# First two tiles' output projection inside the attention's last steps, in the banks of the maxima; the last head group's copies by whole bank

## The chip, the cores and the metric

The kernel runs on one core of a Trainium2 chip. The metric is the device time of one execution in microseconds (us); a figure for the kernel is the median of several executions. Five engines work in parallel: TensorE (PE, with PEld for its weight loads), VectorE (DVE), ScalarE (ACT), GpSimd (POOL) and SyncE (SP), which here issues all DMAs of the stretch that matters. Each engine takes its instructions in the order in which they are written for it.

## The reference

The reference is a transformer block on 2048 tokens with 640 features: sliding window attention with 32 heads of 20 features and a window of 256, then a gated MLP whose gate mixes tokens.

```python
qkv = (layernorm(x) @ wqkv)                      # 32 heads of 20
scores = einsum("bhqd,bhkd->bhqk", q, k) * 20 ** -0.5
p = softmax(where(0 <= i - j < 256, scores, -1e9))
h = x + einsum("bhqk,bhkd->bhqd", p, v) @ wo
z = gelu(layernorm(h) @ w_in); z1, z2 = halves(z)
g = w_sp @ layernorm(z2) + b_sp                  # over tokens
out = h + (z1 * g) @ w_out
```

## The kernel before

The work is fp32 in quality: operands are split into a high and a low part (hi, lo), and each product takes three matmuls (hi·hi, hi·lo, lo·hi). Tokens lie in 16 tiles of 128. The order of the instructions on PE, DVE, ACT and SP is that of the code; only POOL is scheduled by the framework.

The attention runs as 128 steps `u`: eight groups `g` of four heads, and in a group 16 blocks of 128 keys. Step `s` of the loop holds, four times (`hh`, one for each head of the group):

- `max_item` for step `s + 16` (scores for the row maxima; PE fills a bank, DVE reduces it into `junk`), as long as there are steps left, so it is missing in the last 16;
- `score_item` for step `s`: PE fills a bank with scores, ACT takes the exponential into `pt` (line 392), and after the fourth head POOL masks `pt` (lines 394 and 397);
- at `hh` 1 and 3 `pv_item` for step `s - 2`: PE multiplies `pt` with V into a PSUM tile `pv` (line 415), one tile for each 512 tokens of a group, two buffers. After every second key block one half (256 tokens) of a `pv` tile is final; it is copied to `ot` by ACT (line 427) or DVE (line 429) and stored to `o_d` in HBM (line 430). Row 20 of each head holds the softmax sums.

PSUM has eight banks: two for `pv`, six as `bank0` to `bank5` in two rings. Ring 1 (three banks) is that of the maxima; when these end, one of its banks goes to ring 2, the scores'. The other two stand idle from then on.

In the last steps a generator `proj_early`, advanced once a step, prepares the output projection: `load_o(j)` loads tiles 2j and 2j+1 of the attention's result from `o_d` into `m1` (line 157, four DMAs) and the sums into `rs` (line 152); `inv` takes the reciprocals (line 192), `norm_o` multiplies (line 162), `split_o` makes hi (a cast, line 168) and lo (a subtraction, line 171), and `load_x2` loads the residual rows `xh` (line 141). For tokens from 512 on the sums are inverted once for all by `inverse_sums`, one generator for each 512 tokens: it loads the sums into `inv` (line 367), takes the reciprocals (line 371) and stores them to `r_d` (line 372), from which `rs` is loaded later.

The projection of a tile (`proj_o`, line 100) is 30 matmuls. For tiles 0 and 1 it is issued in the two steps after the last score, in new PSUM tiles `wo_ps`, opened when the six banks are closed. After the loop, step `i` of the next stage projects tile `i` on PE, then transposes the normalised rows of tile `i - 2` (`turn_h`, `ht_ps`, line 825); DVE adds the residual (`add_h`, line 1198) and takes the statistics (line 1204), POOL three small operations (lines 85 to 87), and ACT writes the normalised rows `hn` (line 91).

Much later, `second_gate(p)` (p from 0 to 7) runs the second half of the token mixing: PE products `g` (line 1036), to which DVE adds what `first_gate` had left in `g_d`. The load of `g_d[p]` into the row `gi` is issued with the pair's first product.

Of the kernel before, what the change touches and what calls it, by code (L numbers as in the profile page):

```python
# [7 lines left out]
F32 = mybir.dt.float32  # L8
# [3 lines left out]
OP = mybir.AluOpType  # L12
# [3 lines left out]
P = 128  # L16
# [18 lines left out]
def block_kernel(ctx, tc, x, wqk, wv, wo, w_in, wsp, bsp, w_out, out):  # L35
# [5 lines left out]
    def pool(stack, name, **kw):  # L41
        return stack.enter_context(tc.tile_pool(name=name, bufs=1, reuse_waits="tile", **kw))
# [96 lines left out]
    def load_x2(i):  # L139
        hs[i] = mem["xh"][i % 5]  # L140
        nc.sync.dma_start(hs[i], x[i * P:(i + 1) * P, :])

    def load_o(j, sums=False):

        t = slice(2 * j * P, (2 * j + 2) * P)
        ot, rs = m1(j % 2 * 2 * D, KD, 2 * P), mem["rs"][j % 2]
        for i in range(2):
            ots[2 * j + i] = (ot[:, :, i * P:(i + 1) * P], rs[:, i * P:(i + 1) * P])

        def load_rs(sums=False):  # L150
            base, step = (o_d[:, DH, t], 32 * S) if sums else (r_d[:, t], S)
            nc.sync.dma_start(rs, bass.AP(tensor=base.tensor, offset=base.offset, ap=[[0, 4], [step, H], [1, 2 * P]]))

        if sums:
            load_rs(True)
        for d in range(4):
            nc.sync.dma_start(ot[32 * d:32 * d + 32], o_d[:, d:4 * KD:4, t])
        return load_rs

    def norm_o(i):  # L160
        ot, rs = ots[i]
        nc.vector.tensor_tensor(out=ot, in0=ot, in1=rs[:, None, :].to_broadcast([P, KD, P]), op=OP.mult)

    def split_o(i, on_dve=False):
        ot, _ = ots[i]
        hi, lo = ots[i] = mem["osp"][i % 3]
        if on_dve:
            nc.vector.tensor_copy(out=hi, in_=ot)
        else:
            nc.scalar.activation(hi, ot, AF.Copy)  # L170
        return lambda: nc.vector.tensor_tensor(out=lo, in0=ot, in1=hi.bitcast(F32), op=OP.subtract)

    def proj_o(i, ps):
        osp = ots.pop(i)
        wo_s = mem["wo"]
        gemm(ps, HD, [lambda k, p=p: osp[p][:, k, :] for p in range(2)],
             [lambda k, j, p=p: wo_s[p][:, k, j * HD:(j + 1) * HD] for p in range(2)], KD)
        return ps

    def proj_early():  # L180
# [22 lines left out]
        lo = split_o(0, True)  # L203
        load_x2(1)
        yield
        lo()
        norm_o(1)
        load_x2(2)
        yield
        split_o(1, True)()  # L210
        rs = load_o(2)
        yield
        inv(1)
        load_x2(3)
        yield
        load_x2(4)
        norm_o(2)
        lo = split_o(2, True)
        yield
        lo()  # L220
        norm_o(3)
        yield
        yield
        rs()


    with ExitStack() as ab:
# [50 lines left out]
        def s2_tile():  # L278
            return s_tile(2)
# [80 lines left out]
        def inverse_sums(t0, n):  # L360
            t = mem["inv"][len(inverse) % 2][:, :n // 4]

            def rows(d, step):
                return bass.AP(tensor=d.tensor, offset=d.offset, ap=[[step, H], [n // 4, 4], [1, n // 4]])

            yield
            nc.sync.dma_start(t, rows(o_d[:, DH, t0:t0 + n], 32 * S))
            yield
            yield
            yield  # L370
            nc.vector.reciprocal(out=t, in_=t)
            nc.sync.dma_start(rows(r_d[:, t0:t0 + n], S), t)
            yield
# [26 lines left out]
        def pv_item(u):  # L400
            g, kb = divmod(u, NT)
            pt = p_tiles.pop(u)
            a, e = kb * P, min(S, kb * P + 384)
            mid = (a // 512 + 1) * 512 if a // 512 < (e - 1) // 512 else a + 192
            for a, b in ((a, min(mid, e)), (mid, e)):
                if a >= b:
                    continue
                c = a // 512
                first = (g, c) not in pv_tiles
                if first:  # L410
                    pv_tiles[g, c] = pv_tile(f"pv{g}_{c}")
                ps = pv_tiles[g, c]
                for hh in range(4):
                    v0 = 21 * (4 * g + hh)
                    nc.tensor.matmul(ps[32 * hh:32 * hh + 32, a - 512 * c:b - 512 * c],  # L415
                                     v_sb[:, kb, v0:v0 + 32], pt[:, hh, a - kb * P:b - kb * P],
                                     start=first, stop=(kb == 4 * c + 3), skip_group_check=True,
                                     tile_position=(0, 32 * hh))
                if b < e:
                    yield  # L420
            c = kb // 4
            for j in (kb // 2 % 2,) if kb % 2 else ():
                ps = pv_tiles.pop((g, c)) if j else pv_tiles[g, c]
                ot = tmp3.tile([P, 256], F32, tag="ot", bufs=6, name=f"ot{g}_{c}_{j}")
                src, e = ps[:, 256 * j:256 * j + 256], c * 512 + 256 * j
                if u >= NU - 2 or j == 0 and u < NU - LEAD:
                    nc.scalar.activation(ot, src, AF.Copy)
                else:
                    nc.vector.tensor_copy(out=ot, in_=src)  # L429
                nc.sync.dma_start(o_d[4 * g:4 * g + 4, :, e:e + 256].rearrange("h d t -> (h d) t"), ot)  # L430
            if g == 7 and kb % 4 == 3 and c:
                inverse.append(inverse_sums(c * 512, 512))
# [200 lines left out]
        b1.close()  # L633
        tmp3 = pool(x01, "tmp3", side="right")
        early, pre_ps = None, []
        for s in range(NU + 2):
            if s % NT == 0 and s < 6 * NT:
                ld = load_stack(s // NT + 2)
            for _ in range(1 + s % 2):
                next(ld, None)  # L640
            u1 = s + LEAD
            for hh in range(4):
                if u1 < NU:
                    max_item(u1 // NT, u1 % NT, hh)
                if s < NU:
                    score_item(s, hh)
                if hh == 1 and u1 % 8 == 0 and s <= NU - LEAD:
                    rows = max_rows((u1 - 8) // NT, (u1 - 8) % NT // 8)
# [24 lines left out]
            for f in inverse:  # L673
                next(f, None)
        for _ in early:
            pass


    psK = ctx.enter_context(ExitStack())
# [152 lines left out]
    def at(n, f):  # L832
        later.setdefault(n, []).append(f)
# [289 lines left out]
    def second_gate(p):  # L1123
# [71 lines left out]

    def add_h(i):
        h3 = hs[i].rearrange("p (a b) -> p a b", a=2)
        nc.vector.tensor_tensor(out=h3, in0=pre_ps.pop(0)[:, :, :HD], in1=h3, op=OP.add)
        nc.sync.dma_start(h_d[i], hs[i])

    def bn_h(i):
# [94 lines left out]
```

## Time and profile before

| | us |
|---|---|
| three runs | 1128.23, 1132.79, 1138.03 |
| median | 1132.79 |
| profiled execution | 1131.8 |
| its span, first to last instruction | 1130.1 |

The profile gives PE 1095.6 us busy (97% of the span), DVE 725.6, ACT 567.3 and POOL 313.0, with 28703 instructions. It comes as a page and as answers to questions on the trace. A row of the timeline has the start in us from the span's start, the time busy, the engine, the line, the operation, the tiles (out<-in), and in brackets the idle time before it with what ended it. SPq rows are DMA issues. A row of the windows has, for each engine, busy us and instructions, then the granted TensorE clock as a share of full speed, the busy share of the DMA engines and GB/s. A row of the chain of waits has a start, a length and what the end hung on there.

### The profile page before, as it was taken

Reading aid. Unit: us, or ns where it says so; the run is one execution under the profiler, and the core shown is the slowest. Engines: PE = TensorE matmul, PEld = TensorE weight load, DVE = VectorE, ACT = ScalarE, POOL = GpSimd, SP = SyncE. Lnnn points to the kernel's source line nnn. Section 1 sums busy time; section 2 is a strip of 40 time slices with the busy share of each in tenths; the row PEclk is TensorE's granted clock in tenths of the full one; section 3 lists DMA queues with packets and bytes.
Section 4 is the critical chain, followed back from the end, with each engine's and each line's share of the span. In section 5 each row is a group of like instructions: output and inputs, shape, how many; then the busy total and the mean of one; then the engine's idle time right before and its main releaser. Section 6 shows DMA issues by size and latency. Waiting matters only on the chain.

```text
span 1130.1 us, 28703 instructions
## 1 busy us (share of the span) xinstructions
PE 1095.6 (97%) x11180; PEld 988.7 (87%) x11180; DVE 725.6 (64%) x2013; ACT 567.3 (50%) x1198; POOL 313.0 (28%) x477
## 2 busy tenths in 40 slices
PE   8999999999999999699999999999999999999998
PEld 7998887667778877499999999999999899999998
DVE  5541213788989998568777678556358974566542
ACT  4433443248989999635566567333247521222210
POOL 4424444446667667623300012000002100000000
PEclk9999999999999999999999999999999999999999
DMA  6622446555555555679754522233251564444322
GB/s 198 211 70 72 143 136 243 170 179 167 180 181 178 183 177 160 169 214 304 262 177 168 178 90 75 85 122 96 97 170 52 169 187 145 135 136 147 98 76 78
DMA packets 82168, 171.78 MB, mean 152 GB/s; under 512 B 10816, under 2 KB 43072, under 8 KB 78144
## 3 DMA queue, kind: packets, MB, share of 16 engines
q1 hardware_dynamic: 82032, 169.95, 47.0%
q8 instruction: 88, 1.44, 0.6%
q14 instruction: 48, 0.39, 0.1%
HBM read 112.04 MB, written 57.87 MB: 150 GB/s over the span
## 4 chain that ended last, share of the span: by engine, by line
PE 51%; ACT 3%; DVE 2%; DMA 2%; issue 1%; POOL 1%; SPq 0%; ACTq 0%; DVEq 0%; POOLq 0%
PE g L1036 22%; PE out_ps L1101 8%; PE wo_ps L100 6%; PE zb L937 5%; PE zx L885 2%; PE zv L885 2%; PE zy L885 1%; PE zw L885 1%; PE yt_ps L1090 1%; ACT pt L392 1%; DVE row L696 1%; PE ht_ps L825 1%; PE out_l L1101 1%; DMA o_d<-ot 1%; DVE zl L696 0%
## 5 line engine op out<-in xcount | busy, mean ns | idle before, releaser
L392 ACT ACTIVATE pt<-bank 128x384 f32<-128x384 f32 (+2 forms) x512 | 202.0, 489 | 24.3 <-PE bank L390 19.3
L702 ACT ACTIVATE aw<-fx 128x512 fp32r<-128x512 f32 (+2 forms) x160 | 93.3, 595 | 167.9 <-PE g L1036 113.1
L1036 PE MATMUL g<-zl,aw 128*128 128x432 f32 x768 | 171.3, 359 | 0.7 <-ACT zl L702 0.4
L338 DVE CUSTOM_DVE_ANT_0 junk<-bank,strip 128x288 bf16<-128x288 f32 x392 | 156.1, 454 | 13.5 <-PE bank L328 10.5
L1036 PEld LDWEIGHTS g<-zl,aw 128*128 128x128 f32 x768 | 143.8, 188 | 8.1 <-ACT zl L702 1.5
L415 PE MATMUL pv<-pt,v_sb 128*32 128x192 f32 (+3 forms) x1984 | 130.7, 324 | 13.3 <-DVE ot L429 7.7
L1036 PE MATMUL g<-ze,aw 128*128 128x432 f32 x576 | 134.2, 362 | 2.2 <-DVE row L696 1.6
L696 DVE TENSOR_TENSOR aw<-fx,aw 128x512 fp32r<-128x512 f32 (+2 forms) x160 | 102.7, 646 | 38.2 <-ACT aw L702 36.6
L1036 PEld LDWEIGHTS g<-ze,aw 128*128 128x128 f32 x576 | 107.9, 189 | 7.9 <-ACT y_sp L136 1.2
L390 PE MATMUL bank<-slot 123*32 123x288 bf16 (+7 forms) x1536 | 108.5, 275 | 2.5 <-ACT pt L392 1.5
L394 POOL TENSOR_SCALAR_AFFINE_SELECT pt<-pt 128x512 f32<-128x512 f32 x128 | 83.1, 649 | 64.3 <-ACT pt L392 62.9
L1101 PE MATMUL out_ps<-wout,y_sp 128*128 128x320 f32 (+1 forms) x630 | 96.7, 310 | 0.4 <-ACT y_sp L136 0.4
L1101 PEld LDWEIGHTS out_ps<-wout,y_sp 128*128 128x128 f32 (+1 forms) x630 | 94.0, 188 | 2.1 <-ACT y_sp L136 1.1
L937 PE MATMUL zb<-win,aw 128*128 128x432 f32 x480 | 95.4, 359 | 0.0
L937 PEld LDWEIGHTS zb<-win,aw 128*128 128x128 f32 x480 | 89.9, 187 | 5.0 <-ACT row L702 0.3
L328 PE MATMUL bank<-slot 120*32 120x288 bf16 (+6 forms) x1280 | 90.0, 274 | 1.5 <-DVE mcol L338 1.5
L85 POOL TENSOR_SCALAR mvz<-mvz 128x1 f32<-128x1 f32 x16 | 5.0, 315 | 292.5 <-DVE mvz L84 283.5
L527 DVE TENSOR_TENSOR rest<-qk,sg 128x512 f32<-128x512 f32 x40 | 27.7, 692 | 84.2 <-ACT sg L525 84.2
L415 PEld LDWEIGHTS pv<-pt,v_sb 128*32 128x32 f32 x1984 | 61.1, 110 | 22.1 <-issue 19.1
L696 DVE TENSOR_TENSOR row<-g,row 128x432 f32<-128x432 f32 x80 | 48.1, 604 | 45.9 <-PE g L1036 42.5
L390 PEld LDWEIGHTS <-slot 123*32 123x32 bf16 x1728 | 60.6, 97 | 17.7 <-issue 9.0
L397 POOL TENSOR_SCALAR_AFFINE_SELECT pt<-pt 128x512 f32<-128x512 f32 x112 | 72.9, 651 | 0.0
(182 smaller groups left out, 2212.0 us busy)
## 6 DMA issues: line engine op xcount, KB each, us to landing
slot<-qk_d SPq DMA_DIRECT2D x144, 160.0 KB
fx<-wsp_in SPq DMA_DIRECT2D x32, 512.0 KB
qk_d<-sg SPq DMA_DIRECT2D x40, 384.0 KB
fx<-hn_d SPq DMA_DIRECT2D x32, 320.0 KB
o_d<-ot SPq DMA_DIRECT2D x64, 128.0 KB
xb<-qk_d SPq DMA_DIRECT2D x48, 160.0 KB
z_d<-row SPq DMA_DIRECT2D x16, 432.0 KB
g_d<-row SPq DMA_DIRECT2D x16, 432.0 KB
```

Of the source, the lines that this page charges most:

```text
L328: nc.tensor.matmul(ps[32 * j:32 * j + 32, o:o + w], one(st, 120, 0, hh, q0, 32), k, start=True, stop=True, tile_position=(0, 32 * j))
L338: nc.vector.tensor_tensor_reduce(out=junk[:, :n], in0=ps[:, :n], in1=keep, scale=1.0, scalar=NEG, op0=OP.add, op1=OP.max, accum_out=m_cols ...
L390: nc.tensor.matmul(ps[32 * i:32 * i + 32, b + o:b + o + w], one(st, 123, 1, hh, k0, 32), q, start=True, stop=True, tile_position=(0, 32 * i))
L392: nc.scalar.activation(pt[:, hh, :n], ps[:, :n], AF.Exp, scale=SCALE)
L394: nc.gpsimd.affine_select(out=pt[:, :, :P], in_=pt[:, :, :P], pattern=[[0, 4], [1, P]], base=0, channel_multiplier=-1, compare_op=OP.is_ge ...
L397: nc.gpsimd.affine_select(out=pt[:, :, 256:], in_=pt[:, :, 256:], pattern=[[0, 4], [-1, P]], base=-1, channel_multiplier=1, compare_op=OP. ...
L415: nc.tensor.matmul(ps[32 * hh:32 * hh + 32, a - 512 * c:b - 512 * c], v_sb[:, kb, v0:v0 + 32], pt[:, hh, a - kb * P:b - kb * P], start=fir ...
L696: (eng or nc.vector).tensor_tensor(out=out, in0=a, in1=b, op=op)
L702: nc.scalar.activation(out, a, AF.Copy)
L937: nc.tensor.matmul(b[0][:, :HF], a[t][:, x, kk], win2[0][:, y, kk, h * HF:(h + 1) * HF], start=kk + x + y == 0, stop=kk == KD - 1 and x == 1)
L1036: nc.tensor.matmul(ps, w[m][:, x, k], zc[k][m][:, y], start=start and k + x + y == 0, stop=stop and k == 3 and x == 1, skip_group_check=True)
L1101: nc.tensor.matmul(ps[j][:, :HD], src[:w, a, k, :], e1["wout"][:w, b, k, j * HD:(j + 1) * HD], start=(k == 0 and a + b == 0), stop=(k == K ...
```

## The change

Five edits, in the code's order:

1. Tiles 0 and 1 are projected by a generator `proj_two` of single matmuls (`proj_steps`). From step NU - 6 on, one matmul follows each head's items (24 in six steps); in the two steps after the last score, four do. Tile 0 writes the two banks left in ring 1 (`bank0`, `bank2`), tile 1 two banks of ring 2. The six banks are no longer closed for new tiles there, and `add_h` of these two tiles reads two single banks.
2. In group 7, from token 512 on, both halves of a `pv` tile are copied after its last key block, not the first half two steps earlier. The last tile's two copies are both ACT's.
3. `proj_early` is reordered: hi and lo of a tile directly after each other, the reciprocals of the second pair later, `load_o(2)` two steps later, the loads of `xh` around them.
4. `inverse_sums(512, 512)` takes its reciprocals one step earlier.
5. `second_gate(p)` for p over 0 issues the load of `g_d[p]` three steps earlier.

```diff
+    def proj_steps(i, ps):
+        osp = ots.pop(i)
+        wo_s = mem["wo"]
+        for k in range(KD):
+            for a, b in ((0, 0), (0, 1), (1, 0)):
+                for j in range(2):
+                    nc.tensor.matmul(ps[j][:, :HD], osp[a][:, k, :], wo_s[b][:, k, j * HD:(j + 1) * HD], ...)
+                    yield
...
-            for j in (kb // 2 % 2,) if kb % 2 else ():
+            if g < 7 or c == 0:
+                halves = (kb // 2 % 2,) if kb % 2 else ()
+            else:
+                halves = (0, 1) if kb % 4 == 3 else ()
+            for j in halves:
...
+        def proj_two():
+            for i in range(2):
+                ps = ring[1] if i == 0 else [s2_tile(), s2_tile()]
+                yield from proj_steps(i, ps)
+                pre_ps.append(ps)
...
-                if hh == 2 + s - NU and s >= NU:
-                    if s == NU:
-                        psB.close()
-                        psW = pool(psB, "psW", space=PSUM)
-                    pre_ps.append(proj_o(s - NU, psW.tile([P, 2, 512], F32, tag="wo", bufs=3, name=f"wo_ps{s - NU}")))
+                if s >= NU - 6:
+                    for _ in range(1 if s < NU else 4):
+                        next(two_tiles, None)
...
-            yield
+            if t0 > 512:
+                yield
             nc.vector.reciprocal(out=t, in_=t)
...
-        at(n0 - (0 if p else 1), lambda: nc.sync.dma_start(gi, g_d[p]))
+        at(n0 - (3 if p else 1), lambda: nc.sync.dma_start(gi, g_d[p]))
```

On TensorE, in step NU - 6, the first moved matmul (line 186 of the changed kernel; `bank0` is tile 0's first half, `xb0` its hi) stands here; line 400 is scores, 390 before:

```order
L400 LDWEIGHTS slot1_1_1954
L400 MATMUL bank5_120<-slot1_1_1954 32x288
L186 MATMUL bank0_115<-xb0_93 128x320
L400 LDWEIGHTS slot1_1_1954
L400 MATMUL bank3_118<-slot1_1_1954 32x288
```

Before, the scores of `bank3` followed those of `bank5` directly; the first matmul of tile 0 came after step NU's first `pv`.

On VectorE, around the first projections, the order before was this; `xb0` and `xb1` hold hi and lo of the tiles, `ot7_c_j` is the copy of half j of tokens 512c to 512c + 511, and `rs1` the sums of tiles 2 and 3:

```order
L192 RECIPROCAL rs0_9409<-rs0_9409 128x256
L162 TENSOR_TENSOR m1_9406<-m1_9406,rs0_9409 128x5x128
L168 CAST xb0_93<-m1_9406 128x640
L429 COPY ot7_1_1_9756<-pv7_1_9542 128x256
L171 TENSOR_TENSOR xb0_93<-m1_9406,xb0_93 128x640
L162 TENSOR_TENSOR m1_9406<-m1_9406,rs0_9409 128x5x128
L168 CAST xb1_94<-m1_9406 128x640
L171 TENSOR_TENSOR xb1_94<-m1_9406,xb1_94 128x640
L429 COPY ot7_2_0_9831<-pv7_2_9717 128x256
L192 RECIPROCAL rs1_9410<-rs1_9410 128x256
```

A copy stood between hi and lo of tile 0, and the next behind all of tile 1's.

In the changed kernel VectorE has, from the same place on (line numbers are its own; L202 and L381 are the reciprocals of `rs` and `inv`, L443 is the copy):

```order
L171 TENSOR_TENSOR xb1_94<-m1_9406,xb1_94 128x640
L202 RECIPROCAL rs1_9410<-rs1_9410 128x256
L381 RECIPROCAL inv1_9412<-inv1_9412 128x128
L443 COPY ot7_2_0_9913<-pv7_2_9714 128x256
L443 COPY ot7_2_1_9916<-pv7_2_9714 128x256
L162 TENSOR_TENSOR m1_9406<-m1_9406,rs1_9410 128x5x128
L168 CAST xb0_93<-m1_9406 128x640
L171 TENSOR_TENSOR xb1_94<-m1_9406,xb0_93 128x640
L162 TENSOR_TENSOR m1_9406<-m1_9406,rs1_9410 128x5x128
L381 RECIPROCAL inv0_9411<-inv0_9411 128x128
L1222 TENSOR_TENSOR xh0_9413<-bank0_115,xh0_9413 128x320
```

The copies of `ot7_2` now stand behind the reciprocal of `inv1` and ahead of tile 2's hi and lo; the reciprocal of `inv0` still stands right ahead of the first `add_h`.

SyncE's queue in the changed kernel (L157 loads attention results, L444 stores copies, L376 loads sums), from the loads of tiles 2 and 3 to the load that `inv0` waits for:

```order
L157 DMA m1_9406<-o_d_64 32x5x256 x4
L141 DMA xh0_9413<-x_in 128x640
L141 DMA xh1_9414<-x_in 128x640
L444 DMA o_d_64<-ot7_1_0_9754 128x256
L444 DMA o_d_64<-ot7_1_1_9757 128x256
L141 DMA xh2_9415<-x_in 128x640
L376 DMA inv1_9412<-o_d_64 128x1x128
```

The store of `ot7_1_0` stood ahead of the loads of `xh0` and `xh1` before and stands behind them now; the load of `inv1` stood behind `load_o(2)` and stands ahead of it now. Further on in the same queue:

```order
L382 DMA r_d_66<-inv1_9412 32x4x128
L444 DMA o_d_64<-ot7_2_0_9913 128x256
L444 DMA o_d_64<-ot7_2_1_9916 128x256
L152 DMA rs0_9409<-r_d_66 128x1x256
L141 DMA xh4_9417<-x_in 128x640
L376 DMA inv0_9411<-o_d_64 128x1x128
```

Both stores of `ot7_2` now stand behind the store of `inv1`'s reciprocals, and `rs0` and `xh4` have come between them and the load of `inv0`.

More of the change, by code (lines that the diff above doesn't have):

```diff
@@ L178, in proj_o @@
         return ps
+    def proj_steps(i, ps):
[4 more added lines that the diff above has]
+                for j in range(2):
+                    nc.tensor.matmul(ps[j][:, :HD], osp[a][:, k, :], wo_s[b][:, k, j * HD:(j + 1) * HD],
+                                     start=(k + a + b == 0), stop=(k == KD - 1 and a == 1))
+                    yield
     def proj_early():
@@ L202, in proj_early @@
         norm_o(0)
-        lo = split_o(0, True)
+        split_o(0, True)()
         load_x2(1)
         yield
-        lo()
         norm_o(1)
+        split_o(1, True)()
         load_x2(2)
         yield
-        split_o(1, True)()
-        rs = load_o(2)
         yield
         inv(1)
+        yield
+        rs = load_o(2)
         load_x2(3)
         yield
+        norm_o(2)
+        split_o(2, True)()
+        yield
+        rs()
         load_x2(4)
-        norm_o(2)
-        lo = split_o(2, True)
         yield
-        lo()
         norm_o(3)
         yield
-        yield
-        rs()
     with ExitStack() as ab:
@@ L369, in inverse_sums @@
             yield
-            yield
+            if t0 > 512:
+                yield
             nc.vector.reciprocal(out=t, in_=t)
@@ L674, in block_kernel @@
                 next(f, None)
-        for _ in early:
-            pass
+        for f in (early, two_tiles):
+            for _ in f:
+                pass
     psK = ctx.enter_context(ExitStack())
@@ L1197, in add_h @@
         h3 = hs[i].rearrange("p (a b) -> p a b", a=2)
-        nc.vector.tensor_tensor(out=h3, in0=pre_ps.pop(0)[:, :, :HD], in1=h3, op=OP.add)
+        ps = pre_ps.pop(0)
+        if i < 2:
+            for j in range(2):
+                nc.vector.tensor_tensor(out=h3[:, j], in0=ps[j][:, :HD], in1=h3[:, j], op=OP.add)
+        else:
+            nc.vector.tensor_tensor(out=h3, in0=ps[:, :, :HD], in1=h3, op=OP.add)
         nc.sync.dma_start(h_d[i], hs[i])
```

1 line of the change is left out of this document (added).

## The prediction

> **What bounds the kernel now.** I read the stretches first, since PE is busy 97% of the span: where is the rest, and is it in reach of the change? The last attention steps and the first projections are these rows:
>
> ```profile
> 460.00:465.00 5.00, 4.53 (x114) 3.00 (x107) 4.04 (x5) 5.00 (x14) 4.38 (x7) 1.00 0.23 62
> 465.00:470.00 5.00, 1.16 (x25) 0.64 (x20) 4.93 (x6) 1.39 (x4) 3.10 (x4) 0.95 1.07 232
> 470.00:475.00 5.00, 4.87 (x108) 4.17 (x99) 4.02 (x6) 4.18 (x14) 3.59 (x4) 0.71 0.89 245
> 475.00:480.00 5.00, 1.13 (x17) 0.44 (x17) 2.02 (x3) 0.28 (x2) 1.88 (x3) 0.98 0.88 237
> 480.00:485.00 5.00, 5.00 (x25) 5.00 (x26) 0.95 (x1) 0.00 (x0) 0.00 (x0) 0.68 0.28 90
> ...
> 490.00:500.00 10.00, 10.00 (x72) 9.99 (x71) 7.36 (x13) 4.29 (x7) 3.04 (x6) 1.00 0.97 292
> ```
>
> Up to 465 us ACT is the bound (5.00 of 5.00). Then PE stands twice, and twice the granted clock is down (0.71, 0.68) when it starts again. From 485 us on PE is full. The PE timeline names the holes:
>
> ```profile
> 461.62 0.52 PE L390 MATMUL bank<-slot 123*32 123x288 bf16 x8
> 461.95 0.51 PE L415 MATMUL pv<-pt,v_sb 128*32 128x192 f32 x8
> 462.28 0.62 PE L390 MATMUL bank<-slot 123*32 123x288 bf16 x8
> 462.72 0.51 PE L415 MATMUL pv<-pt,v_sb 128*32 128x192 f32 x8
> ...
> 469.25 0.87 PE L415 MATMUL pv<-pt,v_sb 128*32 128x256 f32 x8 [3.84 <-DVE ot L429]
> ...
> 470.30 0.73 PE L415 MATMUL pv<-pt,v_sb 128*32 128x128 f32 x8
> 470.73 0.78 PE L390 MATMUL bank<-slot 123*32 123x288 bf16 x8
> 471.21 0.73 PE L415 MATMUL pv<-pt,v_sb 128*32 128x128 f32 x8
> ...
> 479.40 0.57 PE L415 MATMUL pv<-pt,v_sb 128*32 128x192 f32 x8 [3.70 <-DVE ot L429]
> ...
> 480.60 0.74 PE L100 MATMUL wo_ps<-xb,xb 128*128 128x320 f32 x2
> 481.14 1.27 PE L100 MATMUL wo_ps<-xb 128*128 128x320 f32 x4
> ```
>
> Both holes (3.84 and 3.70) wait for a copy of half a `pv` bank that sits in DVE's queue behind work for the projection. The chain of waits shows what that work hung on, and where the stage goes afterwards:
>
> ```profile
> 465.40 6.27 DMA o_d<-ot
> ...
> 474.30 3.70 DMA inv<-o_d
> ...
> 478.03 0.95 DVE inv L371
> ...
> 479.97 6.06 PE wo_ps L100 x30
> 486.04 0.47 PE pv L415 x16
> 486.50 9.00 PE wo_ps L100 x60
> 495.50 0.55 PE ht_ps L825 x5
> ```
>
> So a tile costs 4.5 us of PE (9.00 for 60 matmuls, 0.15 each), the first one 6.06: the low clock costs it 1.56. The end hung on DMA round trips. My yardstick is 495.50, the first `turn_h`: it stands behind tile 2 on PE, and PE is full from there.
>
> **What the change removes.** Edit 2 takes both holes away: no half is copied while the other is still to be written. At most that is 3.84 + 3.70 + 1.56 = 9.1 us, and about 0.5 more for the first low clock (a pair of `pv` and scores goes from 0.77, 461.95 to 462.72, to 0.91, 470.30 to 471.21, over 3.4 us). Edit 1 moves 60 matmuls, 24 of them into steps whose bound is ACT.
>
> **What it adds first: a wait for tile 0.** The first moved matmul stands behind the scores of step NU - 6, issued at 461.62, so PE reaches it at about 461.8. It needs tile 0's hi:
>
> ```profile
> 462.68 0.82 DVE L162 TENSOR_TENSOR m<-m,rs 128x640 f32<-128x640 f32 x1 [0.83 <-DMA m<-o_d]
> 463.53 0.82 DVE L168 CAST xb<-m 128x640 fp32r<-128x640 f32 x1
> 464.27 0.41 DVE L429 COPY ot<-pv 128x256 f32<-128x256 f32 x1
> ```
>
> Nothing ahead of that cast moves (its loads are issued as before), so hi is there at 464.35 and PE stands 2.55 us, with scores, `pv` and thereby ACT queued behind it. From 464.4, eleven half steps remain. At the old pace (0.77) they end at 472.9, if the 24 matmuls hide; if none does, 3.6 later; with the clock low for a window, some 1.5 more: 472.9 to 478.0. Then come 36 moved matmuls (5.4) and two `pv` (about 1.0), then tile 2 (4.5): PE is through with tile 2 between 483.8 and 488.9; I take 484.5. The cost of switching between the full array and the 32-column tiles is not shown by this trace; it lies inside this range or in the cover named next.
>
> **What is late next: the sums' round trips.** `turn_h(0)` needs `hn` of tile 0, and DVE's queue has the reciprocal of `inv0` ahead of `add_h(0)`, in both kernels. The rows that carry this chain:
>
> ```profile
> 453.01 0.34 SPq L430 DMA_DIRECT2D o_d<-ot  x1
> 454.98 0.61 SPq L152 DMA_DIRECT2D rs<-o_d  x1
> ...
> 471.75 2.46 SPq L157 DMA_DIRECT2D m<-o_d  x4
> ...
> 476.61 0.36 SPq L430 DMA_DIRECT2D o_d<-ot  x1
> ...
> 480.92 0.56 SPq L367 DMA_DIRECT2D inv<-o_d  x1
> ```
> ```profile
> 483.18 0.95 DVE L371 RECIPROCAL inv<-inv 128x128 f32<-128x128 f32 x1 [3.93 <-DMA inv<-o_d]
> 486.08 0.82 DVE L1198 TENSOR_TENSOR xh<-wo_ps,xh 128x640 f32<-128x640 f32 x1 [1.94 <-PE wo_ps L100]
> ```
> ```profile
> 489.89 0.92 ACT L91 ACTIVATE hn<-xh,mvc 128x640 f32<-128x640 f32 x1 [2.30 <-POOL mvc L87]
> ```
>
> They give the prices. A store to `o_d` is readable 1.97 us after its issue in a quiet queue (453.01 to 454.98), 4.31 (476.61 to 480.92) or 6.27 in a full one. A load of `inv` takes 2.26 (480.92 to 483.18) quiet, 3.70 loaded. From the landing of `inv0` to `hn`: 490.81 less 483.18 is 7.63, of which 1.94 waited for PE; with tile 0 projected long before, 5.7.
>
> Now the new order, step by step. Both halves of `ot7_1` are copied after tile 0's lo, at about 466. Their stores stand behind `xh0` and `xh1`, 640 KB. If those cost nothing the stores are readable at 471.75, as before; if all of it goes first, at the stretch's 232 GB/s, 2.8 later, 474.5. I take 473.2. The load of `inv1`, now ahead of `load_o(2)`: 2.5, to 475.7 (bounds 2.26 and 3.70). Reciprocal 0.95, two copies of 0.4, so 477.5; tile 2's hi follows two operations of 0.82 later, 479.2, in time for PE. The second store of `ot7_2` is issued at 477.9; between 1.97 and 4.31, I take 3.0: 480.9, since `load_o(2)` and `xh3` are under way. The issues of `rs0` and `xh4` stand ahead of the load of `inv0`: 0.5, so 481.4; with their 448 KB ahead of it the load takes 3.0 (2.26 to 3.70): **`inv0` at 484.4**, 1.2 later than the 483.18 of now. Then `hn` at 490.1, and `turn_h(0)` there.
>
> **The sum.** 495.50 less 490.1 is 5.4 gained. PE stands from 484.5 to 490.1, longer than the two holes of now, so I charge one low clock, 1.56: net 3.8. Behind it PE is full again; VectorE's chain is only about 1 us ahead of now, but `add_h(1)` need no longer wait for PE, so tiles 4 and 5 are ready in time. Edit 5 has its own row:
>
> ```profile
> DVE row L696 <- DMA row<-g_d: 1.1, 1, 1.1
> PE g L1036 <- DVE row L696: 0.9, 1, 0.9
> ```
>
> That is 1080 to 1090 us; three steps of lead cover a wait of 1.1, and the row's previous user is done by then, so 0.9 goes. The two half `add_h` instead of one are nothing: they lie in DVE's 5.7. Sum: -4.7, from the profiled 1131.8 to 1127.1. The median of the runs stands 1.0 above that execution, with a spread of 10; I give half of it: **1127.5**.
>
> Two bounds for the chain: every price at its quiet end (471.75, 2.26, 1.97, 2.26) gives `inv0` at 480.9 and `hn` at 486.6, a gain of 8.9, less 1.56 or nothing for a gap of 2.1 us, plus 0.9: 1122.0 to 1123.6. Every price at its loaded end (474.5, 3.70, 4.31, 3.70) gives `inv0` at 488.9 and `hn` at 494.6, so 0.9 - 1.56 + 0.9: 1131.6.
>
> **A rule weighed.** Does a short gap cost the clock? This trace says yes: ahead of the low clock of 880 to 890 us PE stood 0.70 us at once, with two shorter holes just before:
>
> ```profile
> 880.00:890.00 10.00, 8.70 (x35) 7.25 (x34) 8.40 (x16) 7.15 (x13) 1.55 (x3) 0.83 0.50 170
> ```
> ```profile
> 885.37 2.04 PE L1036 MATMUL g<-ze,aw 128*128 128x432 f32 x6 [0.70 <-DVE row L696]
> ```
>
> [...]
>
> **The rivals.**
> - *The forecast*, the chain as priced: 1127.5, chance 0.40.
> - *The quick chain*: stores and loads at their quiet prices, because `load_o(2)` no longer stands ahead of `inv1`. For it speaks that the queue was empty at 462 us and (0.28) at 480 us; against it the 1.07 and 0.89 in between. About 1122.5; if PE alone sets the end, tile 2 at 483.8 and no low clock, 495.50 - 483.8 + 0.9 gives 1119.2. Chance 0.25, of it 0.09 under 1121.5.
> - *Ring order*: small stores wait for the whole loads ahead of them, at each of the three round trips: the loaded ends, 1131.6. For it speaks the 6.27 of a 128 KB store behind 640 KB of `m`. Chance 0.18. [...]
> - *The next stage gives it back*: from 490 us on the DMA engines are 0.97 busy; if they set that stage's end, only edit 5's 0.9 and perhaps 1 remain: 1130.5. Against it: PE is 10.00 of 10.00 there, DMA waits for PE's results. Chance 0.10.
> - *Slower: the clock stays down.* The wait for tile 0's hi halves the clock, and the mixed stream, broken by waits, does not bring it back before tile 3. Then six steps cost 12 half pairs of 0.91 and 24 matmuls of 0.27 (480.60 to 481.14 for two), 17.4, so 481.8; 36 matmuls 9.7 and two slow `pv` 0.9, 492.4; tile 2 8.1: 500.5, 5.0 later than 495.50, and tile 3 3.6 more: 1139.5 with edit 5. Against it: in the same mix the clock came back within one window after 469.25. Held through tiles 4 and 5 as well it passes 1%, 1146.7. Chance 0.07, of it 0.03 over 1% slower.
>
> That the change does not do what it says, that is, that ACT-bound steps have no room for PE, is inside the forecast: up to 488.9 the cover of the chain hides it.
>
> **The numbers.** The range holds the first four cases without the best third of the quick one and takes in both ends of the chain, with a little for the spread of the runs: 1121 to 1133.5. One per cent, 11.3 us, is about what a measurement of this kernel can tell from no change. Faster by more: 0.10; slower by more: 0.03; the rest 0.87.
>
> **What would show it.** In the profile after: no wait of `pv` for `ot` over 1 us; a wait of about 2.5 us of the first moved matmul for DVE at 461.8; a wait of the first transposes `ht_ps` of 4 to 6 us, ended by ACT's `hn` near 490, with a low clock behind it; `inv0` as the load DVE waits for longest. If the transposes do not wait, the chain was quick; if PE waits for tile 2's cast instead, `inv1` was late. A wait in 500 to 560 us would be the fourth case. The prediction fails if a buffer of PSUM that I took for free is held longer.

## The result, and the profile after

The changed kernel is **slower**, by a little under 1%: 1144.71 us (median of 22 executions) against 1134.15 beside it, ratio 1.0084 (95% interval 1.0063 to 1.0104). The forecast was 1127.5, the range 1121.0 to 1133.5. The profiled execution took 1144.58 us, span 1142.9 (before: 1131.8 and 1130.1), at a mean granted clock of 0.984 (before: 0.995). Of the 22 executions, 21 had a clock of 0.982 to 0.991 and took 1140.33 to 1149.97 us; one had 0.998 and took 1130.68. The ratios leave out executions more than 1.5% above the fastest of the same kernel (one of 3787.44 us of the kernel before among them), so that they come out a little low for a kernel whose executions fall into two groups; the single times of such kernels are given below.

The stretches of the changed kernel (length, then busy time of PE, PEld, DVE, ACT, POOL, then granted clock, DMA share and GB/s):

```profile
460.00:465.00 5.00, 4.31 (x104) 2.64 (x95) 1.76 (x2) 5.00 (x15) 3.95 (x7) 1.00 0.60 158
465.00:470.00 5.00, 3.27 (x31) 1.48 (x31) 4.86 (x8) 1.82 (x5) 1.70 (x2) 0.77 0.63 142
470.00:475.00 5.00, 5.00 (x40) 2.07 (x36) 2.35 (x2) 1.97 (x5) 1.53 (x2) 0.50 1.01 244
...
485.00:490.00 5.00, 5.00 (x41) 2.18 (x37) 2.78 (x3) 1.53 (x4) 2.46 (x3) 0.50 0.38 107
490.00:500.00 10.00, 10.00 (x71) 6.27 (x72) 1.96 (x6) 1.11 (x4) 1.66 (x4) 0.58 0.01 2
500.00:510.00 10.00, 10.00 (x76) 9.61 (x75) 7.12 (x13) 4.87 (x8) 2.12 (x5) 1.00 0.54 162
```

Read the clock column against the PE column. PE is "busy" 5.00 of 5.00 from 470 us on, so nothing seems to be wrong with it, yet the clock is down to 0.50 and stays there past 490 us. The instruction count gives it away: 40 in 5 us, where the row of 460 to 465 has 104, and where the same stream at full clock has 63 (f1_nowait, below). Before, the same stage had two low stretches of 0.71 and 0.68 and was back at 0.98 between them. Read by the half microsecond, each of the two lasts 3.4 us, from 469.5 to 472.9 and from 479.8 to 483.2, and the one of the changed kernel 30.7 us, from 467.7 to 498.4. The rows at the ends, of the first one before and then of that after (0.53 is a clock of 0.50 for 0.47 of the 0.5 us):

```profile
469.50:470.00 0.50, 0.50 (x12) 0.32 (x8) 0.50 (x1) 0.00 (x0) 0.00 (x0) 0.53 1.20 151
...
472.50:473.00 0.50, 0.50 (x11) 0.28 (x6) 0.47 (x2) 0.50 (x2) 0.50 (x1) 0.56 0.56 179
```
```profile
467.50:468.00 0.50, 0.50 (x9) 0.29 (x1) 0.50 (x3) 0.42 (x1) 0.00 (x0) 0.65 0.96 299
...
498.00:498.50 0.50, 0.50 (x4) 0.50 (x4) 0.50 (x2) 0.00 (x0) 0.00 (x0) 0.63 0.00 0
```

The waits of PE from 440 to 515 us begin with these:

```profile
PE bank L186 <- DVE xb L168: 2.3, 1, 2.3
PE bank L400 <- ACT pt L402: 1.3, 2, 1.1
PE pv L425 <- ACT ot L441: 0.3, 1, 0.3
```

The holes of 3.84 and 3.70 us are gone, and the first moved matmul waits 2.3 us for tile 0's hi. The PE timeline shows what follows that wait:

```profile
464.15 0.31 PE L400 MATMUL bank<-slot 123*32 123x288 bf16 x4
466.73 0.42 PE L186 MATMUL bank<-xb 128*128 128x320 f32 x1 [2.27 <-DVE xb L168]
467.07 0.31 PE L400 MATMUL bank<-slot 123*32 123x288 bf16 x4
467.21 0.50 PE L425 MATMUL pv<-pt,v_sb 128*32 128x192 f32 x8
467.64 0.64 PE L186 MATMUL bank<-xb 128*128 128x320 f32 x1
468.20 0.43 PE L400 MATMUL bank<-slot 123*32 123x288 bf16 x4
468.56 0.64 PE L186 MATMUL bank<-xb,xb 128*128 128x320 f32 x1
469.13 0.43 PE L400 MATMUL bank<-slot 123*32 123x288 bf16 x4
469.34 0.85 PE L425 MATMUL pv<-pt,v_sb 128*32 128x192 f32 x8
...
493.54 0.87 PE L425 MATMUL pv<-pt,v_sb 128*32 128x192 f32 x8
494.34 1.17 PE L186 MATMUL bank<-xb 128*128 128x320 f32 x3
495.31 0.73 PE L186 MATMUL bank<-xb,xb 128*128 128x320 f32 x2
...
498.47 0.46 PE L186 MATMUL bank<-xb,xb 128*128 128x320 f32 x2
...
507.68 0.71 PE L846 MATMUL ht_ps<-ident,hn 128*128 128x128 f32 x5
```

Behind the wait each single moved matmul holds PE for 0.56 us (467.64 to 468.20). From the `pv` of 467.21 to that of 493.54 there are eleven half steps: 26.33 us, 2.39 each, where a half step took 0.77 before. The clock comes back only when moved matmuls stand together, five (494.34 to 495.98) and then eight (from 496.77), and the scores between them are over, at 498.4: two of them then take 0.39 (498.47 to 498.86, where `pv` follows) in place of 0.67 (495.31 to 495.98).

The stage ahead of this one ends at a slightly different time in each execution, so stages are compared from one common row, the last `pv` before 457 us that waits 0.2 us for POOL (453.13 before, 455.66 after). From there to `turn_h(0)` it is 42.21 us before (495.34) and 52.02 after (507.68): **9.8 us lost**, while 2.5 of the 12.8 us between the two spans were there already. To the first matmul of the next stage, `zx`, it is 110.36 (563.49) and 120.38 (576.04). All kernels below are read by this second length. Each is that of one profiled execution: for e4_four it was the fastest of its ten, for g4_bursts4 the slowest, and for g1_firstonly and g3_half, whose executions fall into two groups, one with the low clock.

| kernel | `pv` at | first `zx` at | length | against before |
|---|---|---|---|---|
| before | 453.13 | 563.49 | 110.4 | |
| after | 455.66 | 576.04 | 120.4 | +10.0 |
| e1_none | 453.13 | 562.49 | 109.4 | -1.0 |
| e2_late | 451.01 | 560.20 | 109.2 | -1.2 |
| e3_one | 453.70 | 562.53 | 108.8 | -1.5 |
| e4_four | 451.33 | 557.65 | 106.3 | -4.0 |
| f1_nowait | 452.47 | 559.06 | 106.6 | -3.8 |
| f2_pairs | 450.88 | 561.50 | 110.6 | +0.3 |
| f3_addfirst | 452.75 | 561.87 | 109.1 | -1.2 |
| f4_banks | 452.05 | 559.50 | 107.5 | -2.9 |
| g1_firstonly | 455.68 | 577.47 | 121.8 | +11.4 |
| g2_from5 | 452.98 | 561.32 | 108.3 | -2.0 |
| g3_half | 453.34 | 574.05 | 120.7 | +10.3 |
| g4_bursts4 | 456.53 | 565.92 | 109.4 | -1.0 |

### The profile page after: what moved, and what is told of

The parts are those of the page before. It is cut to its first block, busy times and chain, and to the rows that moved or that the text cites. A ratio compares the mean times of both kernels' runs of the same rounds, so it can differ in the third digit from the quotient of the medians.

```text
span 1142.9 us, 28702 instructions
## 1 busy us (share of the span) xinstructions
PE 1112.4 (97%) x11180; PEld 991.2 (87%) x11180; DVE 724.7 (63%) x2014; ACT 569.6 (50%) x1199; POOL 311.5 (27%) x477
## 4 chain that ended last, share of the span: by engine, by line
PE 48%; DVE 4%; ACT 3%; DMA 2%; POOL 1%; issue 1%; SPq 0%; DVEq 0%; POOLq 0%; ACTq 0%
PE g L1057 22%; PE out_ps L1122 8%; PE zb L958 3%; PE wo_ps L100 3%; PE zx L906 2%; PE bank L186 2%; PE zv L906 2%; PE zy L906 1%; PE zw L906 1%; DVE row L717 1%; PE yt_ps L1111 1%; PE pv L425 1%; ACT row L91 1%; PE bank L400 1%; DVE aw L717 1%
## 5 line engine op out<-in xcount | busy, mean ns | idle before, releaser
L402 ACT ACTIVATE pt<-bank 128x384 f32<-128x384 f32 (+2 forms) x512 | 204.6, 488 | 39.8 <-PE bank L400 33.8
L425 PE MATMUL pv<-pt,v_sb 128*32 128x192 f32 (+3 forms) x1984 | 133.2, 331 | 5.0 <-ACT ot L441 3.5
L400 PE MATMUL bank<-slot 123*32 123x288 bf16 (+7 forms) x1536 | 111.7, 282 | 3.0 <-ACT pt L402 2.1
L337 PE MATMUL bank<-slot 120*32 120x288 bf16 (+6 forms) x1280 | 92.3, 277 | 1.6 <-DVE mcol L347 1.5
L400 PEld LDWEIGHTS <-slot 123*32 123x32 bf16 x1728 | 58.4, 97 | 22.0 <-issue 13.6
```

The lines of the kernel that those rows point to most:

```text
L337: nc.tensor.matmul(ps[32 * j:32 * j + 32, o:o + w], one(st, 120, 0, hh, q0, 32), k, start=True, stop=True, tile_position=(0, 32 * j))
L400: nc.tensor.matmul(ps[32 * i:32 * i + 32, b + o:b + o + w], one(st, 123, 1, hh, k0, 32), q, start=True, stop=True, tile_position=(0, 32 * i))
L402: nc.scalar.activation(pt[:, hh, :n], ps[:, :n], AF.Exp, scale=SCALE)
```

## The experiments

**The theory**: two things together cost the time. The wait for tile 0's hi brings the clock down; full-array matmuls that stand singly between 32-column tiles then keep it down. Rivals: the stream alone does it; the wait alone does it; or it is the new order of copies and loads. Unless said otherwise each kernel is the changed one with the edit shown. The changed kernel itself was not run again beside these; each has the kernel before beside it.

**e1_none**: nothing moved ahead of the last score.

```
-                if s >= NU - 6:
-                    for _ in range(1 if s < NU else 4):
+                if s >= NU:
+                    for _ in range(4):
```

> The 24 matmuls of steps NU - 6 to NU - 1 are issued after the last score instead; the banks, the whole-bank copies and VectorE's order stay as changed. Theory (the wait of 2.27 us for tile 0's hi halves the clock, and single full-array matmuls among the 32-column ones hold it down): no wait, no low clock of more than one window (3.4 us), time about 1128. Rival 1 (the mixed stream alone lowers the clock): the same, about 1128, since the stream is gone. Rival 2 (the new order of copies, loads and reciprocals costs the time): still above 1140.

1130.33 us against 1132.28 of before, ratio 0.9989 (0.9972 to 1.0007). The loss is gone with the interleaving, all other edits in place; the order of copies and loads falls as its cause. What shows up instead, on PE and on DVE:

```profile
492.24 1.33 PE L846 MATMUL ht_ps<-ident,hn 128*128 128x128 f32 x5 [5.76 <-ACT hn L91]
```
```profile
486.15 0.95 DVE L381 RECIPROCAL inv<-inv 128x128 f32<-128x128 f32 x1 [4.80 <-DMA inv<-o_d]
```

This is the "late next" of the prediction: PE is through at 486.48 (492.24 less 5.76) and stands 5.76 us for `hn`, whose addition is queued behind a reciprocal that waits for its load. A low clock follows (0.55 in 490 to 495 us).

**e2_late**: single matmuls, but only from step NU - 4, when tile 0's hi is there.

```
-                if s >= NU - 6:
+                if s >= NU - 4:
```

> The single matmuls start two steps later, at NU - 4, when tile 0's hi and lo are there: 16 in the attention, no wait ahead of them. Theory: without the wait the clock stays up, 1.0 through the stream, time 1128 to 1131. Rival 1 (the stream alone): the clock falls within two windows and stays at 0.5 until the last scores, 16 x 0.6 + slower pv and scores, time about 1140. Rival 2: above 1140 with the clock up.

1132.52 us, a little above what was expected, ratio 1.0006 (0.9989 to 1.0023). No wait for hi, and the clock stays up (1.00 from 445 to 490 us); its PE timeline gives the price of the stream at full clock:

```profile
464.95 0.39 PE L425 MATMUL pv<-pt,v_sb 128*32 128x128 f32 x8
465.28 0.41 PE L186 MATMUL bank<-xb,xb 128*128 128x320 f32 x1
465.62 0.31 PE L400 MATMUL bank<-slot 123*32 123x288 bf16 x4
465.86 0.41 PE L186 MATMUL bank<-xb 128*128 128x320 f32 x1
466.20 0.31 PE L400 MATMUL bank<-slot 123*32 123x288 bf16 x4
466.33 0.39 PE L425 MATMUL pv<-pt,v_sb 128*32 128x128 f32 x8
```

A half step takes 1.38 us (464.95 to 466.33), 0.61 more than the 0.77 of the old mix. A single moved matmul takes 0.34 (465.28 to 465.62), where one in a dense run takes 0.15. So nothing is hidden: two singles are 0.68, their cost almost whole.

**e3_one**: one moved matmul at the head of step NU - 6, with its wait; the others after the last score.

```
-                if s >= NU - 6:
+                if s >= NU or s == NU - 6 and hh == 0:
```

> One matmul of tile 0 stays at its place in step NU - 6 and keeps the wait of 2.3 us; the other 59 follow the last score. Theory: the clock falls once and is back after one window (3.4 us), as before the change; time 1129 to 1132. If the wait alone is what costs, the clock stays at 0.5 for 30 us here too and the time is above 1140.

1132.26 us, ratio 0.9995 (0.9970 to 1.0020). The wait is there (2.22 us), and the clock falls, but only for one stretch:

```profile
465.00:470.00 5.00, 5.00 (x93) 3.42 (x96) 4.93 (x7) 3.78 (x9) 2.00 (x4) 0.66 1.07 223
470.00:475.00 5.00, 4.87 (x109) 3.19 (x100) 0.55 (x1) 4.40 (x15) 3.96 (x7) 1.00 0.65 183
```

The wait alone is not enough either.

**e4_four**: the same 24 matmuls with the same wait, four in a row once a step.

```
-                if s >= NU - 6:
-                    for _ in range(1 if s < NU else 4):
+                if s >= NU - 6 and (s >= NU or hh == 0):
+                    for _ in range(4):
```

> The same 24 matmuls with the same wait in front, but four at a time, once in a step, after the first head's scores: 6 places of switching instead of 24. Theory (the single switching holds the clock down): the clock falls after the wait and is back within two windows (7 us); time 1130 to 1134. Rival 1 (any stream with these matmuls): 0.5 until the last scores, 1140 or more.

1129.39 us, ratio 0.9982 (0.9962 to 1.0003). The wait is even longer (2.97 us), and the clock is back by 470 us:

```profile
460.00:465.00 5.00, 2.03 (x28) 1.27 (x28) 4.00 (x7) 1.61 (x4) 2.36 (x3) 0.88 0.49 108
465.00:470.00 5.00, 5.00 (x72) 3.29 (x68) 3.59 (x4) 3.22 (x8) 2.58 (x4) 0.78 1.06 223
470.00:475.00 5.00, 5.00 (x102) 3.59 (x91) 1.29 (x3) 4.18 (x12) 2.93 (x5) 1.00 0.56 181
```

Same work in the same steps, behind the same kind of wait: what differs is that the matmuls no longer stand singly.

**f1_nowait**: the stream of the changed kernel without its wait.

```
-                    nc.tensor.matmul(ps[j][:, :HD], osp[a][:, k, :], wo_s[b][:, k, j * HD:(j + 1) * HD],
+                    nc.tensor.matmul(ps[j][:, :HD], osp[a][:, k, :] if i else wo_s[a][:, k, :P], wo_s[b][:, k, j * HD:(j + 1) * HD],
```

> As the changed kernel, but tile 0's 30 moved matmuls take a block of the projection's own weights as their stationary operand in place of tile 0's hi and lo, so they have nothing to wait for (tile 0's part of the output is left out of the computation that way). The same 24 single matmuls stand at the same places from step NU - 6. Theory (the wait brings the clock down, the single matmuls only keep it down): no wait ahead of L186, granted clock 1.00 from 460 to 485 us, a half step of about 1.38 us as in the late stream, ht_ps waits 1 to 4 us for hn; time as the kernel before, 1129 to 1134 us. Rival (24 single matmuls are enough by themselves, the 16 of the late stream were too few): the clock falls to 0.50 some windows after the stream's start, half steps of 2.5 us, 1140 us or more.

1128.90 us against 1133.32, ratio 0.9969 (0.9948 to 0.9990); every one of its ten executions has a clock of 0.995 or more. The row of the full stream, then its first moved matmul and the ends of the same eleven half steps:

```profile
465.00:470.00 5.00, 5.00 (x63) 2.49 (x59) 4.88 (x5) 3.31 (x7) 2.44 (x4) 1.00 1.09 194
```
```profile
461.19 0.41 PE L186 MATMUL bank<-xb 128*128 128x320 f32 x1
461.67 0.50 PE L425 MATMUL pv<-pt,v_sb 128*32 128x192 f32 x8
...
477.60 0.51 PE L425 MATMUL pv<-pt,v_sb 128*32 128x192 f32 x8
```

All 24 singles, no wait, no low clock (1.00 in every row from 440 to 510 us). The rival that the stream is enough by itself falls. The eleven half steps that took 26.33 us in the changed kernel take 15.93 here (461.67 to 477.60).

**f2_pairs**: two after the first and two after the third head of a step, with the wait.

```
-                if s >= NU - 6:
-                    for _ in range(1 if s < NU else 4):
+                if s >= NU - 6 and (s >= NU or hh % 2 == 0):
+                    for _ in range(2 if s < NU else 4):
```

> As the changed kernel, the same 24 matmuls over the same six steps with the same wait, but two after the first and two after the third head of a step instead of one after each. Theory (what keeps the clock down are single matmuls between 32-column tiles, each standing by itself at 0.34 us or more where the second in a row takes 0.15): the wait of 2 to 3 us lowers the clock for one or two windows, then it comes back; half step about 1.2 us; 1129 to 1134 us. Rival (any spreading over the attention keeps the clock down, only the bursts of four were short enough): clock 0.50 for 20 us or more, 1138 to 1145 us.

1130.73 us, ratio 0.9976 (0.9950 to 1.0001). A wait of 2.96 us, then:

```profile
460.00:465.00 5.00, 2.36 (x19) 1.29 (x20) 4.30 (x7) 1.33 (x4) 1.92 (x3) 0.72 0.53 120
465.00:470.00 5.00, 5.00 (x54) 2.47 (x53) 3.19 (x3) 2.51 (x6) 1.23 (x2) 0.59 1.06 231
470.00:475.00 5.00, 5.00 (x81) 2.82 (x74) 1.03 (x2) 4.04 (x9) 2.45 (x4) 1.00 0.39 129
```

Two in a row already let the clock come back, a little later than four do.

**f3_addfirst**: e1_none with tile 0's addition and statistics ahead of the reciprocal of the third group of sums.

```
-            for f in inverse:
+            for f in inverse if s <= NU else inverse[:1] + inverse[2:]:
...
         bn_h(i - 1)
+        if i == 1:
+            next(inverse[1])
```

> As the run without interleaving (no moved matmul before the last score), with one more edit: in VectorE's queue the addition and the statistics of tile 0 (add_h(0), bn_h(0)) stand ahead of the reciprocal of the third group of sums, not behind it. Theory (the transposes waited 5.8 us for hn because that reciprocal waited 4.8 us for its load): VectorE adds tile 0 at about 481.4, hn about 4.8 us later, so ht_ps starts at about 486.6 where PE is through with tile 2, no wait over 1 us and no low clock in 485 to 500 us; 8 us less than without the edit, ratio to the kernel before about 0.991. Rival (the following stage is bound by the loads of the attention's outputs, the DMA engines are over 0.9 busy from 490 us on): the gain is given back in 490 to 560 us, ratio 0.998 to 1.000.

1132.77 us, ratio 0.9987 (0.9969 to 1.0006), as the rival had it. The first step came in part (`ht_ps` at 488.33 with a wait of 2.18, where 486.6 and none over 1 us were expected; the clock at 1.00 from 485 to 500 us), and most of it was gone at the end, as its PE timeline shows:

```profile
488.33 0.74 PE L846 MATMUL ht_ps<-ident,hn 128*128 128x128 f32 x5 [2.18 <-DVE xh L1222]
...
540.40 0.76 PE L846 MATMUL ht_ps<-ident,hn 128*128 128x128 f32 x5 [0.93 <-ACT hn L91]
...
557.19 0.76 PE L846 MATMUL ht_ps<-ident,hn 128*128 128x128 f32 x5 [1.04 <-ACT hn L91]
561.87 1.86 PE L906 MATMUL zx<-zl,aw 128*128 128x432 f32 x6 [2.73 <-ACT ho L723]
```

At `turn_h(0)` it is 6.6 us ahead of before (488.33 - 452.75 = 35.58 against 42.21), at `zx` 1.2. The chain that ended last runs through two loads and a store in between:

```profile
491.56 6.76 DMA rs<-r_d
...
501.55 7.67 DMA h_d<-xh
509.23 7.09 DMA rs<-r_d
```

The DMA engines are 1.01 and 1.07 busy in 490 to 510 us, and PE, coming earlier, waits in small pieces. That the loads of this stage take the gain back is read from this chain and was not tested apart. Part of it can be the edit's own doing: it also moved the store of the third group's reciprocals, issued at 488.72, 3.0 us after their reciprocal started (1.0 in e1_none), and VectorE later stands 2.93 us for the load of such sums. And it is no fixed toll: e4_four comes to `turn_h(0)` 4.2 us earlier than before and is still 4.0 earlier at `zx`.

**f4_banks**: the kernel before with the copies by whole bank alone (its second part).

```
-            for j in (kb // 2 % 2,) if kb % 2 else ():
+            if g < 7 or c == 0:
+                halves = (kb // 2 % 2,) if kb % 2 else ()
+            else:
+                halves = (0, 1) if kb % 4 == 3 else ()
+            for j in halves:
```

> The kernel before with the second part of the change alone: the last group's copies by whole bank. Theory: both waits of pv for ot (3.84 and 3.70 us) and the low clock behind them go, PE is through with tile 2 some 5 to 8 us earlier, but ht_ps then waits 4 to 6 us for hn, whose addition stands behind the reciprocal that waits for its load, with a low clock behind it: 0 to 2 us faster than before, ratio 0.998 to 1.000. Rival (these waits were what bound the stage): 6 to 9 us faster, ratio 0.992 to 0.995.

1129.84 us, ratio 0.9974 (0.9954 to 0.9995): faster than the changed kernel, and by 0.3%, at the edge of what these runs can tell, **faster than before**; a little more than the theory gave, far from the rival. Its holes are gone too, and PE waits 3.95 us for `hn` behind them:

```profile
489.04 1.33 PE L829 MATMUL ht_ps<-ident,hn 128*128 128x128 f32 x5 [3.95 <-ACT hn L91]
```

**g1_firstonly**: the control to f1_nowait. Only the first matmul takes tile 0's hi.

```
+                    ... osp[a][:, k, :] if i or k + a + b + j == 0 else wo_s[a][:, k, :P], ...
```

> The control to the run without a wait: of tile 0's 30 moved matmuls only the first takes tile 0's hi as stationary operand, the other 29 again a block of the projection's weights (tile 0's part of the output is left out of the computation). Theory (the wait, not the operands, made the difference): the wait of 2 to 3 us for the cast is there again, and behind it 0.50 clock for 20 us or more, half steps of about 2.5 us, 1140 to 1146 us. Rival (the weights as stationary operand, or the wait for lo, decided it): clock 1.00 from 470 us on, 1128 to 1132 us.

1136.53 us against 1132.43, ratio 1.0037 (0.9995 to 1.0079), and this median says little, since the executions fall in two groups: five with a clock of 0.984 to 0.989 at 1138.97, 1144.90, 1144.96, 1145.36 and 1147.05 us, five with 0.995 or 0.996 at 1129.38 to 1134.08. The profiled one is of the first group:

```profile
PE bank L186 <- DVE xb L168: 2.4, 1, 2.4
```
```profile
470.00:475.00 5.00, 5.00 (x44) 2.08 (x40) 2.50 (x3) 1.96 (x4) 1.22 (x2) 0.50 1.04 249
```

With the operands of f1_nowait and the wait given back, the clock is held down again, so the operands were not what kept it up there. That it happens in 5 of 10 executions, and in 21 of 22 of the changed kernel, was not expected and is not explained.

**g2_from5** and **g3_half**: the stream of singles later, to shorten the wait.

```
-                if s >= NU - 6:
+                if s >= NU - 5:                              # g2_from5
+                if s >= NU - 5 or s == NU - 6 and hh > 1:    # g3_half
```

> As the changed kernel with its single matmuls, but from step NU - 5 (20 instead of 24), 1.54 us of attention later, so that the wait for tile 0's hi shrinks from 2.3 to 3.0 us to 0.7 to 1.5 us. Theory (the wait must take about half of one of the clock's 3.4 us stretches): the clock stays at 1.00 or falls for one stretch alone; half steps 1.38 us; 1129 to 1134 us. Rival (any wait at the head of the stream is enough): 0.50 for 20 us or more, 1140 us or more.

1129.68 us, ratio 0.9984 (0.9955 to 1.0014). In its profile hi was there in time: no wait at all, clock 1.00 from 455 to 505 us. So it says nothing of a short wait; it repeats f1_nowait with 20 singles and the true operands. One of its ten executions (1139.44, clock 0.992) may have been caught.

> As the changed kernel, but the single matmuls begin after the third head of step NU - 6 (22 instead of 24), 0.77 us of attention later, so that the wait shrinks to 1.5 to 2.2 us, between the changed kernel and the start at NU - 5. Theory (a threshold at about half a stretch): mixed, the clock falls in some executions and not in others, median 1130 to 1142 us with a wide spread. Rival (any wait is enough): all executions at 1140 us or more.

1132.13 us, ratio 0.9987 (0.9958 to 1.0017), in two groups: 1137.91, 1138.99 and 1143.58 us at a clock of 0.985, seven others from 1125.00 to 1133.13 at 0.995 or more. A wait of 1.81 us stands in the profiled one, which took 1143.58:

```profile
470.00:475.00 5.00, 5.00 (x40) 2.07 (x36) 0.61 (x1) 1.76 (x5) 1.22 (x2) 0.50 0.64 182
```

The later the stream starts, the rarer the fall: 21 of 22 (5 of 10 in g1_firstonly) at the changed kernel's place, 3 of 10 two heads later, at most 1 of 10 a whole step later. So few executions do not tell 5 of 10 from 3 of 10, nor 3 from 1. No run shows a threshold: the half stretch of the two theories was the author's guess.

**g4_bursts4**: bursts of four from step NU - 4.

```
-                if s >= NU - 6:
-                    for _ in range(1 if s < NU else 4):
+                if s >= NU - 4 and (s >= NU or hh == 0):
+                    for _ in range(4):
```

> Bursts of four, once a step, from step NU - 4 (16 of the moved matmuls ahead of the last scores), so that tile 0's hi is there in time. Theory: no wait for it, clock 1.00 up to 485 us, PE through with tile 2 about 1 us earlier than with bursts from NU - 6, ht_ps then waits 1 to 3 us for hn: 1126 to 1130 us, ratio 0.995 to 0.998. Rival (the stage behind, whose loads keep the DMA engines over 0.9 busy, takes the gain back): ratio 0.999 to 1.001.

1131.38 us, ratio 0.9986 (0.9967 to 1.0005); a miss. No wait for hi, but `ht_ps` waited 6.85 us for `hn`, with a clock of 0.57 in 495 to 500 us: the low clock now stands behind that wait. Whether its later start or the eight matmuls fewer make a difference to e4_four stays open: -1.0 against -4.0 in the table sets its slowest execution against the other's fastest, and the two intervals overlap.

## Why the prediction was wrong

- **The holes** (3.84, 3.70): right. No wait of `pv` over 0.3 us is left.
- **The wait for tile 0's hi**: right, 2.27 us where 2.55 was given.
- **The eleven half steps: the step that failed.** The forecast gave them 8.5 us, 3.6 more if no matmul hides and 1.5 for one low clock, 13.6 at most (464.4 to 478.0). They took 26.33. Two terms are in it. The first is the price of the moved matmuls: none of them hides, and a single one costs 0.34 at full clock, not 0.15 (e2_late). That alone makes 15.93 of the eleven half steps (f1_nowait), 3.8 more than the 12.1 for matmuls that do not hide. Prices from dense runs were used for matmuls that stand alone; what they cost more between 32-column tiles, 0.19 each, does not lie "inside this range" (that it is a cost of switching was not shown), but "the cover named next" still hides it: in f1_nowait `ht_ps` waits 0.96 us for `hn`. The second, and larger, is the low clock: 10.4 more, where 1.5 was charged. It was taken to last as long as those before the change, 3.4 us, and lasts 30.7, and at the low clock a single matmul costs 0.56, not 0.27. This second term decides: f1_nowait pays the first in full, if without the wait of 2.27, and takes 1128.90, inside the range; the one execution of the changed kernel whose clock stayed up (0.998) took 1130.68, inside it too. The low clock also covers part of what follows: the 36 moved matmuls and the `pv` among them take 9.7 (493.54 to 503.28, where tile 2 starts), not 6.4.
- **The slower rival** had the mechanism, at a chance of 0.07, but for one detail: it had the stream "broken by waits", and PE has none there (5.00 of 5.00). It was ruled unlikely because "in the same mix the clock came back within one window after 469.25" (low until 472.9). That mix was not the same: it had no full-array matmul in it; e3_one has a single one, and there the clock does come back too (1.00 in 470 to 475 us). Its price of 1.45 per half step was 0.94 too low: 10.3 us over eleven. The profiled 1144.58 lies above its 1139.5 by 5.1 only, since the rival kept the clock down through tile 3, and the clock came back at 498.4.
- **The late next, the sums' round trips**: hidden in the changed kernel, where PE is later still, and right where the clock stays up. e1_none has the reciprocal's load at 486.15 (given: 484.4), a wait of 5.76 (5.6) and a low clock behind it (0.55). Whether the quick end's gap of 2.1 us leaves the clock up (1122.0) or not (1123.6) no run settles: behind the 2.18 us that `ht_ps` waits in f3_addfirst it stayed at 1.00, behind the 2.22 and 2.27 us for tile 0's hi it fell, in e3_one (0.66 in 465 to 470 us) and in the changed kernel (0.50).
- **The next stage gives it back** (0.10): seen in f3_addfirst, which came 6.6 us earlier and kept 1.2, not in e4_four, which came 4.2 earlier and kept 4.0. What decides between the two was not tested. The changed kernel itself, being late, cannot show it.
- **Edit 5's 0.9**: wrong load. The SP queue and DVE before, then both in the changed kernel:

```profile
1083.85 0.32 SPq L1152 DMA_DIRECT2D row<-g_d  x1
```
```profile
1087.83 1.12 DVE L696 TENSOR_TENSOR row<-g,row 128x432 f32<-128x432 f32 x2 [1.05 <-DMA row<-g_d]
```
```profile
1096.32 0.32 SPq L1173 DMA_DIRECT2D row<-g_d  x1
```
```profile
1100.60 1.12 DVE L717 TENSOR_TENSOR row<-g,row 128x432 f32<-128x432 f32 x2 [1.36 <-DMA row<-g_d]
```

  L1152 and L1173 are the load of `gj`, which the change left where it was; edit 5 moves that of `gi`, one line above. The prediction's row names the tensor `g_d`, not the line that loads it; of the two loads from it the sum took the wrong one, and the wait did not shrink (1.05 before, 1.36 after).

## What to carry to other kernels

In this kernel the price of a dense run misled. Price a moved matmul by a row in which one stands as it will stand, alone between others of another shape (0.34 us here), not by a dense run (0.15). When a new wait is put ahead of such a thin stream, ask what will bring the clock back afterwards: here it was enough to move the work in runs of two or more (the clock at 1.00 from 470 us on in f2_pairs and e4_four), or behind the point where its operand was there (1.00 throughout in e2_late's stream). And see, one stage further on, whether the engine that comes earlier finds its loads.

## What was not expected of the hardware

- A clock that stays down under a PE that the profile calls busy all the time: 0.50 from 467.7 to 498.4 us, 30.7 us, with PE at 5.00 of 5.00, nine times the 3.4 us of a low stretch before the change. At full clock the same stream does not lower it (1.00 in f1_nowait), so here both states held themselves, and a wait of 2.27 us pushed the kernel from one into the other. In all six profiles in which the first moved matmul waits, for 1.81 to 2.97 us, the clock falls behind it.
- What brings the clock up and down was not found. A single full-array matmul among 32-column tiles takes 0.34 us where one in a run takes 0.15, and the profile draws both as busy. Two of them in a half step leave a clock of 1.00 where it is (f1_nowait) and do not bring one of 0.50 up (the changed kernel). What sets the two states apart was not tested.
